# Another slot table and a longer lag between scores and values in a four-layer attention kernel

## The chip, the cores and the metric

The kernel runs on one core of a Trainium2 chip. The core has TensorE (PE; its weight loads are shown apart as PEld), VectorE (DVE), ScalarE (ACT), GpSimd (POOL) and SyncE (SP, which here issues the DMAs). The metric is the device time of one execution in microseconds; the median over several runs is compared.

## The reference

Four layers in a row on a 2048 x 576 input: multi-head attention A, multi-query attention B, A, B, each with a layer norm before it and a residual added behind it. There are 32 heads of 18 columns. In B all heads share one key and one value head.

```python
x = x + _A_ref(_layernorm(x), A_wqkv, A_wo)      # B: wq, and one wk, wv for all heads
...
scores = jnp.einsum("bhqd,bhkd->bhqk", q, k) * (Dh ** -0.5)
p = _softmax(scores, axis=-1)
o = jnp.einsum("bhqk,bhkd->bhqd", p, v)
return o.transpose(...).reshape(B, S, D) @ wo
```

## The kernel before

The order of all instructions is written out by hand (`manual_schedule`); each engine runs its own list in order, and semaphores hold an instruction until what it reads is there.

A layer has a projection part (queries, keys, values), an attention part and an output projection. The attention part goes through 16 pairs of heads and, in each pair, through four blocks of 512 queries: 64 units `w`, each for one `(p, u)`. The two heads of a pair, a = 0 and 1, use different row groups of PE, so a matmul of one and a matmul of the other run side by side.

A unit holds three strands of work:

- Maxima (`max_mm`, L563, and its matmuls L595). The scores of 128 queries against 512 keys are computed into one of three banks (`mtile`), and VectorE reduces each to a maximum (L602). To save reduces, some tiles are made in two steps: a "d" matmul (L587) gives the difference between two key blocks in one of four banks (`etile`), ACT writes its Relu into the scratch tile `side` (L592), and a later "t" matmul has VectorE add that and take the maximum (L599). When the 32 maxima of a block are there, `max_final` (L717) has VectorE take the negated maximum (`neg`, L719) and GpSimd split it in two parts (`hl`, L184 and L723); `max_store` (L725) has VectorE transpose the split (`tr`, L728) and SP store it, and `max_rows` (L732) has SP load it back as two more rows of the queries in `big`. These maxima are for a block about two units ahead.
- Exps (`exp_mm`, L737). A matmul (L743) gives 128 keys x 512 queries of scores with the maximum already subtracted, in one of the four `etile` banks, and ACT takes the exp (L749) into a score tile. Four of five score tiles come from a pool of 15 (`pt`); every fifth goes into one of three slices of `side` in turn (`side[:, 6 + n_p // 5 % 3]`).
- Values (`pv_cols` L753, `pv_block` L762, matmuls L770). Four score tiles are one block; a matmul of each with 19 columns of values and ones runs in its own column group, and eight blocks add up in the one bank `oacc`, which is then copied out (L184 or L182) and combined later: `o_sum` and `o_mul` on GpSimd, `l_part`, `l_out`, `l_rows`, `o_out` as DMAs on SP, `l_inv` on GpSimd. An fp32 value matmul stands in the profile as two passes.

The order of the three strands within a unit is the table `UNIT`, 32 slots, counted from 0. A slot such as "md" names what head 0 and head 1 do: "e" an exp tile, "m" a maximum, "d" and "t" the two-step maximum. The number behind a slot says how many columns of value work follow it; the slots between two numbers are called a group here, and the value work behind it a run. A unit has 16 exps and 16 maxima per head and 4096 columns of values. The value work trails the scores by `LAG` columns: at the start of a layer the first `LAG` columns are skipped, and they are made up behind the loop. `pv_cols` cuts a run wherever a block of 512 columns ends, and each piece is four matmuls of two passes.

The last unit but one goes by the table `ENDS`, the last by `LAST`. Work on a finished block, DMAs and loads are hung on stages: a stage is four exps of a head pair (eight stages in a unit), and `run_todo` (L844) issues what is due. `SUM_AT`, `NM_AT` and their like are offsets in stages. `CUT` says how many maxima of each head at the start of a unit still belong to the earlier block.

Of the kernel before, what the change touches and what calls it, by code (L numbers as in the profile page):

```python
# [45 lines left out]
LEAD = 14  # L46
NM_AT = 2
ROW_AT = 5
SUM_AT = 3
L_AT = 5  # L50
INV_AT = 8
R_AT = 8
# [9 lines left out]

UNIT = """md ee me 256 mm ee et 384 te em 320 me me ee 320 me em 384 em em md 448 ee em dt 448 me em em 384
          em te 256 me em ee 384 mm de me 384 me em 128"""
LAST = "ee ee 512 " * 8
LAG = 960

CUT = 4  # L70


def slots(text):
    out = []
    for w in text.split():
        if w.isdigit():
            out[-1][1] = int(w)
        else:
            out.append([w, 0])
    return out  # L80


UNIT, LAST = slots(UNIT), slots(LAST)
KINDS = [[w[a] for w, _ in UNIT if w[a] != "e"] for a in range(2)]
assert sum(n for _, n in UNIT) == 4096 and [len(k) for k in KINDS] == [16, 16]


def max_ops(kinds):
    pairs = kinds.count("d")
    rest = [(qc, kb) for qc in range(4) for kb in range(4) if qc >= pairs or kb > 1]  # L90
    seen, ops = {"d": 0, "t": 0}, []
    for k in kinds:
        if k == "m":
            ops.append((k, *rest.pop(0)))
        else:
            ops.append((k, seen[k], 0))
            seen[k] += 1
    assert not rest
    return ops


ENDS = UNIT[:8] + LAST[:10] + [["ee", 0], ["ee", 4096 - 5 * 512 - sum(n for _, n in UNIT[:8])]]
assert [[w[a] for w, _ in UNIT[:8]].count("e") for a in range(2)] == [8 - CUT] * 2
MAX_OPS = [max_ops(k[CUT:] + k[:CUT]) for k in KINDS]
PLAIN = [(i // 2 % 4, i // 8 % 2 * 2 + i % 2) for i in range(16)]
FIRST_SHARED = 3
# [3 lines left out]
def tile_kernel(ctx: ExitStack, tc: tile.TileContext, A_x, A_wqkv, A_wo, B_x, B_wq, B_wk, B_wv, B_wo, out):  # L110
# [66 lines left out]
    def xtile(name, shape=(P, 2, 9, 256), dt=F32R):  # L177
        return pool.tile(list(shape), dt, tag="xx", bufs=1, name=name)
# [223 lines left out]
    for layer in range(4):  # L402
# [350 lines left out]
        def pv_cols(cols):  # L753

            while cols:
                n, c0 = divmod(pv_at[0], 512)
                w = min(cols, 512 - c0)
                pv_block(n, c0, c0 + w)
                pv_at[0] += w
                cols -= w  # L760
# [54 lines left out]
        def at(b, f, *args):  # L815
            todo.setdefault(b, []).append((f, args))

        ns = STEPS * 4 * NPAIR
        for p in range(NPAIR):
            for u in range(4):  # L820
                b = STEPS * (4 * p + u) + STEPS - 1
                if is_a or p or u:
                    at(b + NM_AT, max_store, p, u)
                    at(b + ROW_AT, max_rows, p, u)
                for d, f in ((SUM_AT, o_sum), (L_AT, l_part), (INV_AT, l_inv), (R_AT, l_out), (RB_AT, l_rows),
                             (MUL_AT, o_mul), (O_AT, o_out)):
# [17 lines left out]
        def run_todo(st):  # L844
            for n in sorted(n for n in todo if n <= st):
                for f, args in todo.pop(n):
                    f(*args)
# [10 lines left out]
        side = xtile("side", (P, 9, 512), F32)  # L858
        late, n_e, n_r, n_p = LAG, 0, [0], [0]
        for w in range(4 * NPAIR):  # L860
            p, u = divmod(w, 4)
            more_m = w < 4 * NPAIR - 2
            e_next = [0, 0]
            for kinds, cols in UNIT if more_m else ENDS if w == 4 * NPAIR - 2 else LAST:
                run_todo(LEAD + STEPS * w + sum(e_next) // 4)
# [14 lines left out]
        for st in range(ns, ns + L_AT + 1):  # L880
            run_todo(LEAD + st)
            if st < ns + OUT_AHEAD:
                next(outs)
                pv_cols(LAG - 512 if st == ns else 512)
        tail = [todo.pop(n, []) for n in range(ns + LEAD + L_AT + 1, ns + LEAD + O_AT)]
# [32 lines left out]
```

## Time and profile before

| | us |
|---|---|
| median of 3 runs | 5732.63 (5728.56 to 5733.11) |
| profiled execution | 5727.82 |
| its span, first to last instruction | 5726.0 |
| PE busy | 5630.5 (98%) |
| VectorE busy | 4922.5 (86%) |
| ACT busy | 4890.3 (85%) |
| GpSimd busy | 1746.1 (30%) |

The profile is of one execution. Lines of a timeline have the start in us from the start of the span, the time that the merged instructions cover, the engine, the source line, what is written and read, and the count; in square brackets stands idle time of the engine before it, and what ended it. The granted TensorE clock was 0.998 of full speed over the span.

### The profile page before, as it was taken

What the parts mean: (1) busy time and instruction counts of PE and PEld (TensorE: products, weight loads), DVE (VectorE), ACT (ScalarE), POOL (GpSimd) and SP (SyncE); (2) the same over time, 40 slices, a digit from 0 to 9 for tenths busy, and PEclk for the clock granted to TensorE, in tenths of its full rate; (3) what the DMA queues carried; (4) which work ended last, traced back from release to release, by engine and by line L of the source; (5) the groups of instructions that cost most, each with busy time, mean ns of one, the idle gap of its engine ahead of it and who ended that gap; (6) DMA issues with size and microseconds to landing.
All of it is one profiled execution on the core that took longest, in us unless ns stands there. A gap on an engine that the chain in (4) does not pass through costs nothing.

```text
span 5726.0 us, 151306 instructions
## 1 busy us (share of the span) xinstructions
PE 5630.5 (98%) x59516; PEld 2991.4 (52%) x59516; DVE 4922.5 (86%) x9517; ACT 4890.3 (85%) x9864; POOL 1746.1 (30%) x2236
## 2 busy tenths in 40 slices
PE   9999999999999999999999999999999999999999
PEld 7644444444844444444685444444448444444446
DVE  4699999998699999999647999999977999999995
ACT  2499999999389999999625999999992899999996
POOL 3142323234233232333321332323342333333232
PEclk9999999999999999999999999999999999999999
DMA  6311111111320000001253111111114101010002
GB/s 226 112 44 39 35 39 36 39 36 25 126 68 23 23 21 22 20 23 25 59 193 93 49 36 37 36 38 39 33 37 127 55 23 24 23 24 20 21 16 78
DMA packets 258610, 292.42 MB, mean 51 GB/s; under 512 B 132700, under 2 KB 172892, under 8 KB 248176
## 3 DMA queue, kind: packets, MB, share of 16 engines
q1 hardware_dynamic: 257896, 282.75, 17.5%
q8 instruction: 467, 7.65, 0.6%
q14 instruction: 247, 2.02, 0.1%
HBM read 158.77 MB, written 119.86 MB: 49 GB/s over the span
## 4 chain that ended last, share of the span: by engine, by line
PE 90%; ACT 8%; DVE 1%; POOL 0%; issue 0%; DMA 0%; SPq 0%; DVEq 0%; ACTq 0%; POOLq 0%
PE oacc L770 36%; PE psm L595 22%; PE pse L743 19%; PE psn L262 6%; PE psq L421 6%; ACT pt L749 5%; PE psd L587 2%; ACT side L749 1%; ACT side L592 1%; DVE mx L602 0%; PE ps L254 0%; DMA qk_d<-ev 0%; POOL wsm L211 0%; PE oacc L255 0%; DVE oc L184 0%
## 5 line engine op out<-in xcount | busy, mean ns | idle before, releaser
L602 DVE TENSOR_REDUCE mxd<-psm 128x1 f32<-128x512 f32 x5856 | 3698.8, 683 | 263.2 <-PE psm L595 174.3
L749 ACT ACTIVATE pt<-pse 128x512 f32<-128x512 f32 x6580 | 3565.8, 635 | 156.5 <-PE pse L743 119.7
L595 PE MATMUL psm<-big 62*128 62x512 f32 x7216 | 2490.4, 447 | 7.0 <-DVE mx L602 5.6
L743 PE MATMUL pse<-big 64*128 64x512 f32 x8192 | 2424.5, 434 | 0.6 <-ACT evr L435 0.5
L770 PE MATMUL oacc<-pt,vbuf 128*19 128x192 f32 (+5 forms) x22768 | 1784.2, 356 | 4.1 <-DVE oc L184 3.6
L595 PEld LDWEIGHTS psm<-big 62*128 62x128 f32 x7216 | 1150.8, 184 | 848.9 <-DVE mxd L602 387.9
L743 PEld LDWEIGHTS pse<-big 64*128 64x128 f32 x8192 | 1202.4, 185 | 473.5 <-ACT pt L749 281.9
L770 PE MATMUL oacc<-side,vbuf 128*19 128x192 f32 (+6 forms) x5600 | 1321.3, 355 | 34.3 <-ACT side L749 31.7
L749 ACT ACTIVATE side<-pse 128x512 f32<-128x512 f32 x1612 | 1016.6, 631 | 24.0 <-PE pse L743 17.1
L770 PEld LDWEIGHTS oacc<-pt,vbuf 128*19 128x19 f32 x22768 | 571.2, 97 | 737.4 <-issue 578.4
L184 POOL TENSOR_SCALAR hl<-neg 128x8 fp32r<-128x8 f32 x256 | 50.9, 199 | 2809.4 <-DVE neg L719 2809.4
L599 DVE CUSTOM_DVE_ANT_0 side<-psm,side 128x512 f32<-128x512 f32 x976 | 650.9, 681 | 69.5 <-PE pse L743 64.2
L770 PE MATMUL oacc<-pt,vy 128*19 128x64 f32 (+2 forms) x8128 | 622.5, 343 | 0.0
L592 ACT ACTIVATE side<-psd 128x512 f32<-128x512 f32 x976 | 612.8, 628 | 0.0
L793 POOL TENSOR_TENSOR rl<-lt,mone 128x8 f32<-128x8 f32 x256 | 423.1, 1653 | 380.7 <-DMA lt<-os 380.7
L770 PEld LDWEIGHTS oacc<-side,vbuf 128*19 128x19 f32 x5600 | 363.2, 97 | 221.9 <-issue 136.3
L770 PE MATMUL oacc<-side,vy 128*19 128x192 f32 (+4 forms) x2000 | 438.2, 341 | 31.7 <-ACT side L749 31.7
L587 PE MATMUL psd<-kd,big 54*128 54x512 f32 x976 | 408.9, 419 | 0.0
L429 ACT ACTIVATE ev<-psq 128x512 fp32r<-128x512 f32 (+1 forms) x112 | 67.0, 598 | 325.8 <-PE psq L421 272.4
L806 POOL TENSOR_TENSOR os<-os,rb 96x512 f32<-96x512 f32 x256 | 328.7, 1284 | 19.1 <-DMA rb<-r_d 19.0
L784 POOL TENSOR_TENSOR os<-os,side 96x512 f32<-96x512 f32 x240 | 308.2, 1284 | 20.0
L770 PEld LDWEIGHTS oacc<-pt,vy 128*19 128x19 f32 x8128 | 198.9, 97 | 209.4 <-issue 177.0
(93 smaller groups left out, 3618.6 us busy)
## 6 DMA issues: line engine op xcount, KB each, us to landing
big<-qk_d SPq DMA_DIRECT2D x180, 432.0 KB
qk_d<-ev SPq DMA_DIRECT2D x96, 512.0 KB
qk_d<-ev SPq DMA_DIRECT2D x120, 256.0 KB
rb<-r_d SPq DMA_DIRECT2D x512, 36.0 KB
o_d<-os SPq DMA_DIRECT2D x512, 36.0 KB
m_d<-tr SPq DMA_DIRECT2D x1024, 2.0 KB
o<-o_d SPq DMA_DIRECT2D x64, 256.0 KB
big<-m_d SPq DMA_DIRECT2D x512, 4.0 KB
```

The costliest lines, as they stand in the source:

```text
L262: nc.tensor.matmul(ps, lhs[:, xc, :], wsm[:, wc, h * 288:(h + 1) * 288], start=i == 0, stop=i == len(TERMS) - 1)
L421: nc.tensor.matmul(ps[:n].rearrange("p (u t) -> p u t", u=2)[:, us], w[:, wc, :n], xts[T][:, us, xc, :], start=(xc, wc) == TERMS[0], stop= ...
L587: nc.tensor.matmul(ps, q[b:b + 3 * DH, c0:c0 + P], kds[p if is_a else 0][b:b + 3 * DH], start=True, stop=True)
L592: nc.scalar.activation(r, ps, AF.Relu)
L595: nc.tensor.matmul(ps, q[b:b + KM, c0:c0 + P], k[b:b + KM, kb * 512:(kb + 1) * 512], start=True, stop=True)
L599: nc.vector.tensor_tensor_reduce(out=r, in0=ps, in1=r, scale=1.0, scalar=-3.0e38, op0=OP.add, op1=OP.max, accum_out=mx[:, r0:r0 + 1])
L602: nc.vector.reduce_max(mx[:, r0:r0 + 1], ps, axis=AX.X)
L743: nc.tensor.matmul(e, k[r:r + KE, kc * P:(kc + 1) * P], q[r:r + KE, u * 512:(u + 1) * 512], start=True, stop=True)
L749: nc.scalar.activation(pt, e, AF.Exp, scale=SCALE)
L770: nc.tensor.matmul(oacc[j:j + DH + 1, cs], v_of(kc)[:, 2 * p + a if is_a else 0, :], pts[p, u, i][:, cs], start=kc < 2 and c0 == 0, stop=k ...
L793: nc.gpsimd.tensor_tensor(rl, lts.pop((p, u)), mone, op=OP.pow)
L806: nc.gpsimd.tensor_tensor(t[:96], t[:96], rb[:96], op=OP.mult)
```

## The change

Four things change together. `LAG` goes from 960 to 1152 columns. The slot table is another one, with the same number of each kind of slot: 16 exps, two "d", two "t" and twelve "m" per head, and twelve runs of value work. `SUM_AT` goes from 3 to 4, so that `o_sum` is issued one stage later. And `ENDS` is made by a function from the first ten slots of the table (`CUT_AT`), not from the first eight. As the change describes itself, no value run of the new table reads a score tile of the last four slots.

```diff
-SUM_AT = 3
+SUM_AT = 4
...
-UNIT = """md ee me 256 mm ee et 384 te em 320 me me ee 320 me em 384 em em md 448 ee em dt 448 me em em 384
-          em te 256 me em ee 384 mm de me 384 me em 128"""
+UNIT = """te ee 256 em me 384 et em me 512 et me ee 448 md dm em 384 em me 192 me ee me 192 md em 384
+          me me em 384 em ee te 192 mm ee 384 dm em em 384 me"""
 LAST = "ee ee 512 " * 8
-LAG = 960
+LAG = 1152

 CUT = 4
+CUT_AT = 10
...
-ENDS = UNIT[:8] + LAST[:10] + [["ee", 0], ["ee", 4096 - 5 * 512 - sum(n for _, n in UNIT[:8])]]
-assert [[w[a] for w, _ in UNIT[:8]].count("e") for a in range(2)] == [8 - CUT] * 2
+def ends(first):
+    left, cols = [16 - sum(w[a] == "e" for w, _ in first) for a in range(2)], 4096 - sum(n for _, n in first)
+    assert left[0] == left[1] and [sum(w[a] != "e" for w, _ in first) for a in range(2)] == [CUT] * 2
+    out = [list(x) for x in first]
+    for i in range(left[0]):
+        n = cols if i + 1 == left[0] else min(cols, 512) if i % 2 else 0
+        out.append(["ee", n])
+        cols -= n
+    return out
+
+
+ENDS = ends(UNIT[:CUT_AT])
```

## The prediction

> **What bounds the kernel.** I read the page first, then the busy time in windows, then PE's timeline, and VectorE's and GpSimd's beside it.
>
> ```profile
> span 5726.0 us, 151306 instructions
> PE 5630.5 (98%) x59516; PEld 2991.4 (52%) x59516; DVE 4922.5 (86%) x9517; ACT 4890.3 (85%) x9864; POOL 1746.1 (30%) x2236
> PE 90%; ACT 8%; DVE 1%; POOL 0%; issue 0%; DMA 0%; SPq 0%; DVEq 0%; ACTq 0%; POOLq 0%
> ```
> ```profile
> 1731.15:1826.13 94.98, 93.53 (x1087) 44.91 (x1080) 88.06 (x171) 91.92 (x186) 29.02 (x35) 1.00 0.09 20
> ```
>
> PE carries the chain, but in a stretch of five units (one unit is one pass through the table of 32 slots; the row has length, busy us of PE, PEld, DVE, ACT, POOL, granted clock, DMA) ACT is busy 97% and DVE 93%. So a unit is set by PE's own work plus the places where PE stands for ACT or DVE, and those have to be read one by one. PE's rows:
>
> ```profile
> 804.79 0.50 PE L595 MATMUL psm<-big 62*128 62x512 f32 x1
> ...
> 817.51 0.40 PE L743 MATMUL pse<-big 64*128 64x512 f32 x2
> ...
> 1733.44 0.42 PE L595 MATMUL psm<-big 62*128 62x512 f32 x1
> 1735.31 0.34 PE L770 MATMUL oacc<-side,vbuf 128*19 128x192 f32 x1 [1.45 <-ACT side L749]
> ...
> 1826.13 0.50 PE L595 MATMUL psm<-big 62*128 62x512 f32 x1
> ...
> 1838.10 0.51 PE L770 MATMUL oacc<-pt,vbuf 128*19 128x384 f32 x3
> 1838.76 0.23 PE L770 MATMUL oacc<-pt,vbuf 128*19 128x64 f32 x2
> 1838.99 0.50 PE L595 MATMUL psm<-big 62*128 62x512 f32 x1
> 1839.33 0.39 PE L595 MATMUL psm<-big 62*128 62x512 f32 x1
> 1839.56 0.39 PE L743 MATMUL pse<-big 64*128 64x512 f32 x1
> 1839.89 0.51 PE L770 MATMUL oacc<-pt,vbuf 128*19 128x384 f32 x2
> 1840.66 0.50 PE L743 MATMUL pse<-big 64*128 64x512 f32 x1
> 1841.32 0.23 PE L770 MATMUL oacc<-pt,vbuf 128*19 128x64 f32 x1
> ...
> 1841.88 0.49 PE L595 MATMUL psm<-big 62*128 62x512 f32 x1
> ...
> 1846.29 0.49 PE L595 MATMUL psm<-big 62*128 62x512 f32 x1
> ```
>
> From start to start: a group of three slots takes 0.34 + 0.23 + 0.33 = 0.90 us (1838.99 to 1839.89), one of two 0.66 us (1840.66 to 1841.32), a value run of 384 columns in one piece 0.77 us (1839.89 to 1840.66), one of 256 columns 0.56 us (1841.32 to 1841.88), one of 448 in two pieces 0.89 us (1838.10 to 1838.99); so a run is 0.14 us and 0.00164 us a column. The unit from 1826.13 to 1846.29 takes 20.16 us; taken out of the 94.98 us of five units, the plain ones are 18.70 us. The difference, 1.46 us, is the stand at 1735.31: 1733.44 to 1735.31 is 1.87 us where 0.33 is usual, so 1.54 us there. The view of waits has its kind in the first two lines (us in total, times, longest); the third is used at the end:
>
> ```profile
> PEld oacc L770 <- ACT side L749: 85.5, 73, 1.8
> PE oacc L770 <- ACT side L749: 63.4, 52, 1.5
> PEld psm L595 <- DVE mxd L602: 387.9, 732, 0.9
> ```
> ```profile
> 1734.61 0.65 ACT L749 ACTIVATE side<-pse 128x512 f32<-128x512 f32 x1
> ```
>
> PE waits for an exp that began at 1734.61, the newest one issued. Every fifth exp goes to one of three slices of side, so a slice is sent a new tile 15 exps later; by my count of the old table the run after slot 5 still reads columns 320 to 511 of a tile issued 15 exps before, so it waits for the exp that has just been given that slice. 32 exps a unit and every fifth to side make the pattern come round every five units.
>
> **The change, part by part.** A layer has 62 units by the table, four layers 248.
>
> *The stand.* In the new table the oldest tile that any run reads was issued 14 exps before, so no slice is rewritten under a reader, and by the counted distances no run needs an exp that is not four score tiles back, where the ring of four banks has already forced ACT to be done. 248 / 5 = 50 stands of 1.46 to 1.54 us go: −75 us. The next thing that can be late for a run, the copy of oacc, stands where it did.
>
> *Pieces.* 12 runs, 8 groups of three slots and 4 of two stay (the lone last slot joins the next unit's first two); cut at multiples of 512, the runs make 16 pieces instead of 19. From 384 columns in one piece to 448 in two is 0.12 us, and 64 columns are 0.105, so a further piece costs 0 to 0.02 us. I take 0.005, since starts are read to 0.01: 3 x 248 pieces are −4 us (0 to −15). The Trainium skill, "TensorE: Matmul & The Clock Gate", section "Wait — 56ns, not 53.3ns?", has a fixed 2.5 ns per matmul; a piece is eight matmuls, so that would be an estimated 20 ns and −15 us, and the sum 11 us lower. The rows above allow that only as their upper end.
>
> *VectorE.* The negated maximum (neg, L719) and the transpose of its split (tr, L728) move against the score maxima. Before, two reduces lie between them:
>
> ```profile
> 802.90 0.69 DVE L602 TENSOR_REDUCE mxd<-psm 128x1 f32<-128x512 f32 x1
> 803.62 0.19 DVE L719 TENSOR_REDUCE neg<-mxd 128x8 f32<-128x32 f32 x1
> 803.73 1.28 DVE L602 TENSOR_REDUCE mxd<-psm 128x1 f32<-128x512 f32 x2
> 804.92 0.20 DVE L728 STREAM_TRANSPOSE tr<-hl 128x32 f32<-128x32 f32 x1
> 805.33 0.69 DVE L602 TENSOR_REDUCE mxd<-psm 128x1 f32<-128x512 f32 x1 [0.20 <-PE pse L743]
> ...
> 823.86 0.20 DVE L728 STREAM_TRANSPOSE tr<-hl 128x32 f32<-128x32 f32 x1
> 824.00 1.29 DVE L602 TENSOR_REDUCE mxd<-psm 128x1 f32<-128x512 f32 x2
> ```
> ```profile
> 803.90 0.20 POOL L184 TENSOR_SCALAR hl<-neg 128x8 fp32r<-128x8 f32 x1 [11.26 <-DVE neg L719]
> 804.18 0.20 POOL L723 TENSOR_TENSOR hl<-neg,hl 128x8 fp32r<-128x8 f32 x1
> ```
> The transpose needs GpSimd's second hl, which ends at 804.38, 0.57 us after neg's end (803.81); the two reduces covered that. In the new table neg is issued after slot 8 and the transpose at slot 10 (12 exps issued, stage 3), and slot 9 is "ee": in the changed program's order nothing lies between them in 252 of 256 windows. So VectorE stands from 803.73, when neg lets it go on, to 804.42 (0.04 us after hl, an estimate from the 0.06 shown below for a freed bank): 0.69 us a unit, and every maximum behind it is late. No row of before shows VectorE standing there; that the reduces behind cannot pass the waiting transpose is what the Trainium skill says in "PSUM — Partial Sum Buffer", section "Engine vs sequencer instructions" (the queue is strict FIFO). By that rule the sum is as below; if they could pass, it would be the first rival's.
>
> What PE pays, with time 0 at the start of slot 7: PE is at slot 8 at 0.34, at slot 9 at 0.57, leaves for the 448-column run at 0.90, and is at slots 10, 11, 12 at 1.78, 2.12, 2.35, each with one maximum; the 384-column run from 2.68 ends at 3.46. VectorE starts slot 7's job at 0.54 (804.79 to 805.33), slot 8's at 1.14 (two reduces in a row take 1.29 and one 0.69, so a step is 0.60), neg at 1.86 (0.72, 802.90 to 803.62), which ends at 2.05; hl ends at 2.62, the transpose starts at 2.66 and slot 10's reduce at 2.80 (0.14, 823.86 to 824.00), ending at 3.49; slot 11's ends at 4.09. The ring of three maximum banks binds slot 13 to slot 10 and slot 14 to slot 11. What a freed bank costs is shown on ACT's side, in the first group of a unit:
>
> ```profile
> 1731.88 0.18 PEld L743 LDWEIGHTS pse<-big 64*128 64x128 f32 x1 [0.20 <-ACT pt L749]
> ```
> ```profile
> 1729.71 2.11 ACT L749 ACTIVATE pt<-pse 128x512 f32<-128x512 f32 x4
> ...
> 1732.21 0.59 ACT L749 ACTIVATE side<-pse 128x512 f32<-128x512 f32 x1
> 1732.69 0.60 ACT L749 ACTIVATE pt<-pse 128x512 f32<-128x512 f32 x1
> ```
> ```profile
> 1731.72 0.39 PE L595 MATMUL psm<-big 62*128 62x512 f32 x1
> 1731.88 0.49 PE L743 MATMUL pse<-big 64*128 64x512 f32 x1
> 1732.30 0.39 PE L770 MATMUL oacc<-pt,vbuf 128*19 128x256 f32 x1
> ```
>
> ACT's end 1731.82 to the weight load 1731.88 is 0.06 us, and the run follows 0.42 us later instead of 0.33, so 0.10 more when the load is not hidden. Slot 13 is due at 3.46 and can load at 3.49 + 0.06 = 3.55: 0.09 us. Slot 14 is then due at 3.89 and gets its bank at 4.09 + 0.16 = 4.25: 0.36 us. Together 0.45 us x 248 = +112 us. Bounds: 0, if VectorE's slack (6.9 of 94.98 us above) lay just here, and 0.69 x 248 = 171 us, if none did. I take 0.45, because both waits come out of the chain with durations that are in rows.
>
> *ACT.* In the first group above PE loses 1731.88 − 1731.72 = 0.16 and 0.09 us in the exit to ACT, 0.25 us in every unit. A score tile costs ACT 0.48 us (1732.21 to 1732.69). Tallying 0.48 per exp or Relu against the time of each group and run, with the copy of oacc as one more, ACT's backlog is highest at 0.84 us in the old table (the copy's 0.48, then "me me ee 320" brings four jobs, 1.92, in 0.90 + 0.66) and at 0.81 us in the new (0.24 left of the copy at slot 15, then "me ee me 192" brings 1.92 in 0.90 + 0.45). So I expect these waits at other places and of the same size, smaller by that 0.03 us: −7 us. Bounds: the largest single wait goes, or one more like it comes, ±0.25 x 248 = ±62 us.
>
> *SUM_AT, LAG, the ends.* o_sum goes one stage later on GpSimd, which is busy 30%, so the DMAs on SP behind it (lt, then o_d and the rows of maxima) may go up to 1.7 us later.
>
> ```profile
> 810.03 0.52 SPq L734 DMA_DIRECT2D big<-m_d x2
> ```
>
> The rows are issued 7.5 us before the unit's first exp that needs them (817.51), so that is covered. 192 more columns per layer move behind the loop: 192 x 0.00164 = 0.31 us, four times +1 us, if the loop's start gains nothing. The order of instructions on SP and GpSimd stays, and four oacc copies move from VectorE to ACT, 0.6 us each: nothing.
>
> Sum against the profiled execution, 5727.82 us (span 5726.0 and 1.8 around it; 4.8 us or 0.08% under the median of the runs, 5732.63, which I leave aside): 5727.8 − 75 − 4 + 112 − 7 + 1 = 5755 us.
>
> **Rivals.**
> 1. The removed stand pays and VectorE's hides (other side: faster). VectorE is idle 6.9 of 94.98 us, 1.4 us a unit, twice the 0.69. If the 0.69 us falls into that idle time and delays no bank, the sum loses the 112: 5643 us. Against it: in slots 10 to 14 five maxima follow in a row, and PE issues those slots faster than VectorE's 0.60 us each. It decides where the wait stays under 0.29 us a unit, (5716 − 5643) / 248.
> 2. Cost and gain cancel: a wait of 0.29 to 0.39 us a unit, 5716 to 5739 us.
> 3. VectorE's whole stand reaches PE, or PE's stand at a value run stays, at another place: 5643 + 171 = 5814 us, or 5755 + 75 = 5830 us. For it: VectorE is 93% busy. Against it: the distances counted above, and idle time of VectorE such as the 0.20 us before 805.33.
>
> **How the numbers follow.** The forecast's own case, a wait of 0.39 to 0.60 us, 5740 to 5792 us, gets 0.56; rival 1 0.16; rival 2 0.15; rival 3 0.13. About 0.2% (11 us) is what a measurement can tell from no change. Slower by more: the forecast's case and rival 3, with a little off for their edge, 0.67; within: 0.16; faster: 0.17. The range runs from 5700 to 5800 us: it holds the forecast's case, rival 2 and the edges of the others.
>
> **What would show it.** Right: no value run with idle time of a microsecond before it and a releaser on ACT; five-unit stretches all of one length, near 95.6 us (5 x (18.70 + 0.45 − 0.03 − 0.015)) instead of 94.98, with no long unit in them; VectorE idle before the transpose, about 0.6 us each and released by GpSimd's hl, some 150 us in all; PE's weight loads for maxima waiting for DVE some 100 us more than the 388 of before. Wrong: units of 18.3 to 18.7 us (rival 1), or a long unit every fifth (rival 3), or the first unit's exps waiting for rows of maxima.

## The result and the profile after

The changed kernel takes 5738.64 us (median of 17 runs, 5734.45 to 5745.97) against 5729.64 us (17 runs, 5724.97 to 5734.01) for the kernel before on the same chip: a ratio of 1.0016 with a 95% interval of 1.0009 to 1.0024. It is 9 us slower, inside the 0.2% that the prediction named as no change. The forecast was +27 us; the direction is right and the size is three times too large.

Lines of the changed kernel stand 13 further down than before (the score matmul L743 is L756 now, the value matmul L770 is L783, the exp L762, VectorE's reduce L615, its transpose L741). The page of the changed kernel:

```profile
span 5736.9 us, 139041 instructions
...
PE 5672.8 (99%) x53724; PEld 2800.5 (49%) x53724; DVE 4941.0 (86%) x9513; ACT 4951.8 (86%) x9868; POOL 1741.0 (30%) x2236
...
PE 74%; DVE 21%; POOL 2%; issue 1%; ACT 1%; DMA 0%; POOLq 0%; SPq 0%; DVEq 0%; ACTq 0%
```

The third line is the share of each engine in the chain that ended last. Before, it was PE 90%, ACT 8%, DVE 1%: beside PE, that chain now runs through VectorE and no longer through ScalarE. PE still waits for ScalarE too, as the table of groups below shows. The span grew by 10.9 us.

Busy time in two stretches of five units (start and end, length, then busy us of PE, PEld, DVE, ACT and POOL, granted clock, DMA share, GB/s):

```profile
777.78:872.89 95.11, 94.61 (x965) 41.13 (x961) 88.49 (x171) 93.18 (x187) 28.90 (x35) 1.00 0.15 37
872.89:967.99 95.10, 94.61 (x966) 41.13 (x962) 88.53 (x171) 93.16 (x187) 28.89 (x35) 1.00 0.15 37
```

Five units take 95.1 us, where they took 94.98 and the forecast was 95.6. No unit is long any more: over the 244 units whose twelve runs are all full, every one takes 18.91 to 19.12 us, mean 19.019; before, plain ones took 18.69 and every fifth about 20.2, mean 19.003.

The waits that the prediction spoke of (us in total, times, longest):

```profile
PEld psm L608 <- DVE mxd L615: 427.6, 1220, 0.7
...
PEld psm L608 <- DVE mxd L612: 177.5, 239, 0.7
...
DVE tr L741 <- POOL hl L736: 152.4, 252, 0.6
...
PE oacc L783 <- ACT side L762: 6.8, 4, 1.7
```

The stand of a value run behind a newly issued exp was 63.4 us in 52 places and is 6.8 us in 4. VectorE stands 252 times, 0.6 us each, before a transpose; that row did not exist before. Weight loads for maxima wait 605 us for VectorE's two kinds of reduce (the first two lines), 92 more than the 387.9 + 124.9 of before (the row that the prediction named, plain reduces alone, rose by 40).

One unit from slot 10 to the run behind slot 14, in the timeline of the changed kernel: VectorE first, then GpSimd, then PE and its weight loads (start, time covered, engine, line, what is written and read, idle time before it and what ended that):

```profile
783.83 0.69 DVE L615 TENSOR_REDUCE mxd<-psm 128x1 f32<-128x512 f32 x1
784.55 0.19 DVE L732 TENSOR_REDUCE neg<-mxd 128x8 f32<-128x32 f32 x1
785.35 0.21 DVE L741 STREAM_TRANSPOSE tr<-hl 128x32 f32<-128x32 f32 x1 [0.61 <-POOL hl L736]
785.48 2.44 DVE L615 TENSOR_REDUCE mxd<-psm 128x1 f32<-128x512 f32 x4
```
```profile
785.11 0.20 POOL L736 TENSOR_TENSOR hl<-neg,hl 128x8 fp32r<-128x8 f32 x1
```
```profile
784.43 0.50 PE L608 MATMUL psm<-big 62*128 62x512 f32 x1
...
784.96 0.18 PEld L756 LDWEIGHTS pse<-big 64*128 64x128 f32 x1 [0.23 <-ACT pt L762]
...
785.39 0.25 PE L783 MATMUL oacc<-pt,vbuf 128*19 128x64 f32 x3
...
786.17 0.50 PE L756 MATMUL pse<-big 64*128 64x512 f32 x1
...
786.78 0.18 PEld L608 LDWEIGHTS psm<-big 62*128 62x128 f32 x1 [0.42 <-DVE mxd L615]
...
787.22 0.35 PE L783 MATMUL oacc<-pt,vbuf 128*19 128x192 f32 x2
```

From the start of a group to the start of its run, slots 10 to 12 take 785.39 − 784.43 = 0.96 us, where three slots usually take 0.90, and slots 13 and 14 take 787.22 − 786.17 = 1.05 us, where two usually take 0.66. In the first of them ScalarE is late with one bank (784.96); in the second VectorE is late with the bank of slot 14 (786.78).

Read so for all 244 units, from start to start, the mean of each group of the new table (slots 31, 0 and 1 are the first, since the lone last slot joins the next unit's first two), beside those of three experiments that are told below:

| slots | usual | changed | NM_AT 3 | short exps | short exps, NM_AT 3 |
|---|---|---|---|---|---|
| 31, 0, 1 | 0.90 | 0.982 | 0.988 | 0.984 | 0.978 |
| 10 to 12 | 0.90 | 0.965 | 0.964 | 0.902 | 0.901 |
| 13, 14 | 0.667 | 1.042 | 0.664 | 1.103 | 0.668 |
| 15 to 17 | 0.90 | 0.901 | 1.044 | 0.901 | 0.979 |
| 18, 19 | 0.667 | 0.786 | 0.666 | 0.788 | 0.704 |
| 23 to 25 | 0.90 | 0.976 | 0.954 | 0.973 | 0.982 |
| unit | | 19.019 | 18.664 | 19.021 | 18.577 |

The other groups stand within 0.02 us of the usual.

### The profile page after: what moved, and what is told of

Same layout as the page of the kernel before. It is cut to its first block, busy times and chain, and to the rows that moved or that the text cites. A ratio compares the mean times of both kernels' runs of the same rounds, so it can differ in the third digit from the quotient of the medians.

```text
span 5736.9 us, 139041 instructions
## 1 busy us (share of the span) xinstructions
PE 5672.8 (99%) x53724; PEld 2800.5 (49%) x53724; DVE 4941.0 (86%) x9513; ACT 4951.8 (86%) x9868; POOL 1741.0 (30%) x2236
## 4 chain that ended last, share of the span: by engine, by line
PE 74%; DVE 21%; POOL 2%; issue 1%; ACT 1%; DMA 0%; POOLq 0%; SPq 0%; DVEq 0%; ACTq 0%
PE oacc L783 26%; PE psm L608 18%; PE pse L756 16%; DVE mxd L615 13%; PE psn L275 6%; PE psq L434 6%; DVE side L612 6%; PE psd L600 2%; DVE tr L741 1%; POOL hl L736 1%; DVE neg L732 1%; POOL hl L197 1%; DVE mx L615 1%; PE ps L267 0%; POOLq L197 0%
## 5 line engine op out<-in xcount | busy, mean ns | idle before, releaser
L615 DVE TENSOR_REDUCE mxd<-psm 128x1 f32<-128x512 f32 x5856 | 3645.1, 681 | 129.8 <-PE pse L756 46.6
L762 ACT ACTIVATE pt<-pse 128x512 f32<-128x512 f32 x6580 | 3588.3, 622 | 110.6 <-PE pse L756 58.7
L608 PE MATMUL psm<-big 62*128 62x512 f32 x7216 | 2619.9, 453 | 30.6 <-DVE mx L615 5.0
L756 PE MATMUL pse<-big 64*128 64x512 f32 x8192 | 2465.5, 434 | 4.4 <-ACT pt L762 2.7
L783 PE MATMUL oacc<-pt,vbuf 128*19 128x64 f32 (+6 forms) x20492 | 1797.6, 377 | 3.8 <-DVE oc L197 3.6
L756 PEld LDWEIGHTS pse<-big 64*128 64x128 f32 x8192 | 1213.1, 185 | 904.8 <-ACT pt L762 538.3
L783 PE MATMUL oacc<-side,vbuf 128*19 128x64 f32 (+6 forms) x5044 | 1408.5, 376 | 6.8 <-ACT side L762 6.8
L762 ACT ACTIVATE side<-pse 128x512 f32<-128x512 f32 x1612 | 999.9, 620 | 18.7 <-PE pse L756 7.1
L783 PEld LDWEIGHTS oacc<-pt,vbuf 128*19 128x19 f32 x20492 | 454.2, 97 | 618.2 <-issue 504.7
L605 ACT ACTIVATE side<-psd 128x512 f32<-128x512 f32 x976 | 591.6, 649 | 0.0
L783 PE MATMUL oacc<-pt,vy 128*19 128x384 f32 (+3 forms) x5756 | 587.6, 415 | 0.0
L783 PE MATMUL oacc<-side,vy 128*19 128x384 f32 (+2 forms) x1412 | 456.0, 414 | 0.0
L783 PEld LDWEIGHTS oacc<-side,vbuf 128*19 128x19 f32 x5044 | 319.8, 97 | 157.3 <-issue 124.6
L197 POOL TENSOR_SCALAR os<-side 32x512 f32<-32x512 f32 x480 | 293.6, 612 | 40.0 <-POOL hl L736 0.2
```

The costliest lines, as they stand in the source:

```text
L197: eng.tensor_scalar(dst, src, 1.0, 0.0, op0=OP.mult, op1=OP.add)
L605: nc.scalar.activation(r, ps, AF.Relu)
L608: nc.tensor.matmul(ps, q[b:b + KM, c0:c0 + P], k[b:b + KM, kb * 512:(kb + 1) * 512], start=True, stop=True)
L615: nc.vector.reduce_max(mx[:, r0:r0 + 1], ps, axis=AX.X)
L756: nc.tensor.matmul(e, k[r:r + KE, kc * P:(kc + 1) * P], q[r:r + KE, u * 512:(u + 1) * 512], start=True, stop=True)
L762: nc.scalar.activation(pt, e, AF.Exp, scale=SCALE)
```

## The experiments

**The VectorE stand alone, in the changed kernel.**

```diff
-NM_AT = 2
+NM_AT = 3
```

> The changed kernel with the transpose of the maxima one stage later (NM_AT 3), so that reduces lie between neg and the transpose again. Theory A (VectorE's stand before the transpose makes PE wait at slots 13 and 14, and PE's other waits are ACT's ring of four): the stand of 0.6 us goes, the group of slots 13 and 14 falls from 1.04 to about 0.67 us, some 0.05 of it comes back at ACT's waits, units of 18.64 to 18.75 us instead of 19.02, time 5645 to 5672 us. Rival B (the terms of the prediction simply add up, 0.45 us a unit for VectorE): 5627 us. Rival C (the wait at slots 13 and 14 is ACT's, and VectorE's stand is hidden): 5738 us, no change.

Measured 5649.08 us, ratio to the kernel before 0.9862 (0.9848 to 0.9877): Theory A, and not the 5627 us at which the terms of the prediction would simply add up (Rival B). Slots 13 and 14 fall to 0.664 us, so the whole excess of 0.375 us in that group was VectorE's stand at the transpose. The unit falls by 0.355 us. Behind that group the waits mostly change places: slots 15 to 17 take 0.14 us more, slots 18 and 19 take 0.12 us less. The gain is 88 us.

**The same stand in the old table.**

```diff
-NM_AT = 2
+NM_AT = 1
```

> The kernel before with the transpose one stage earlier (NM_AT 1): in the old table, too, no reduce lies between neg (after slot 7) and the transpose (at slot 8). Theory A: VectorE stands 0.6 to 0.7 us before each transpose, the maxima of slots 8, 9, 11 and 12 are late, and PE pays 0.40 to 0.65 us a unit: 5830 to 5890 us. Rival C (VectorE's 1.4 us of idle time a unit hide the stand): 5730 us.

Measured 5854.67 us, 1.022 (1.0203 to 1.0237), in Theory A's range. The row of the stand appears in the view of waits with nearly the count and length that it has in the changed kernel:

```profile
DVE tr L728 <- POOL hl L723: 151.1, 250, 0.6
```

Plain units go from 18.69 to 19.23 us, so here it costs PE 0.54 us a unit. A transpose too close behind its neg costs 0.36 us a unit in the new table and 0.54 in the old one.

**The stand of the value run alone, in the old table.**

```diff
-            own = n_p[0] % 5 or (p, u) == (NPAIR - 1, 3)
-            pt = pts[p, u, i] = ptile("pt") if own else side[:, 6 + n_p[0] // 5 % 3]
+            own = n_p[0] % 6 or (p, u) == (NPAIR - 1, 3)
+            pt = pts[p, u, i] = ptile("pt") if own else side[:, 6 + n_p[0] // 6 % 3]
```

> The kernel before with every sixth instead of every fifth score tile in the three slices of side, so that a slice is given a new tile 18 exps later and the run after slot 5 reads the tile itself (before, it read the last 192 columns of such a tile from the slice already given to the tile 15 exps later). Theory A (PE's 1.5 us every fifth unit is the wait for the exp just given to that slice): no long units, all at 18.69 us, 5655 us (5645 to 5665). Rival D (ACT is simply that far behind at slot 5 in such units): long units stay, 5725 to 5735 us.

Measured 5649.79 us, 0.9863 (0.9848 to 0.9878), 77 us less than before. A slice of `side` is now sent a new tile 18 exps later, and the long units are gone, five in a row taking 93.41 us instead of 94.98:

```profile
1860.68:1954.09 93.41, 93.41 (x1086) 44.99 (x1080) 87.96 (x171) 91.78 (x186) 28.92 (x35) 1.00 0.09 20
```

So the stand was the rewritten slice, and taking it away is worth what the prediction put down for it. The stand is also a sign of something else: once in five units the kernel before takes, for 192 columns of one score tile, the newer exp that PE has waited for and not the tile that belongs there. The old table with this one edit and the new table with NM_AT 3 are 77 us and more under both kernels, and level with each other.

**The lag alone, backwards.**

```diff
-LAG = 1152
+LAG = 960
```

> The changed kernel with LAG 960, as before: the new table alone. The oldest tile read is then 12 exps old, so no slice is rewritten under a reader; runs read tiles that are as little as 3 exps old. Theory A: no long units, VectorE's stand and the wait at slots 13 and 14 stay, tiles 3 exps old are ready: units of 19.02 us plus 0.01 for more pieces, 5730 to 5745 us. Rival E (the longer lag pays by itself, because fresh score tiles make runs wait for ACT): 0.1 us a unit and more, 5760 us or over.

Measured 6032.18 us, 1.0532 (1.0516 to 1.0547): the main expectation missed by 290 us. One run does it, the 512 columns behind slots 4 to 6, which take 2.21 us instead of 0.99 in every unit. PE and ScalarE there:

```profile
815.98 0.43 PE L783 MATMUL oacc<-pt,vy 128*19 128x320 f32 x1
817.42 0.35 PE L783 MATMUL oacc<-pt,vbuf 128*19 128x192 f32 x3 [1.01 <-ACT side L195]
```
```profile
816.27 0.60 ACT L762 ACTIVATE pt<-pse 128x512 f32<-128x512 f32 x1
816.75 0.62 ACT L195 ACTIVATE side<-oacc 128x512 f32<-128x512 f32 x1
```

With 960 columns a head's last block ends 320 columns into that run. The remaining 192 columns begin the next sum in `oacc`, so they wait for the copy of `oacc` (L195), and the copy stands in ScalarE's queue behind the exps of slots 4 to 6. With 1152 = 256 + 384 + 512 columns the block ends where the run ends, and the copy goes on under the next group's scores. The old table has the same fit at 960 = 256 + 384 + 320. The lag is therefore part of the table, not a choice beside it. The prediction had said that the copy "stands where it did", which is so, but it had priced the lag by the 192 columns at the ends of a layer alone and not seen that the new table needs the longer lag for that.

**The lag alone, in the old table.** To see whether that holds there too:

```diff
-SUM_AT = 3
+SUM_AT = 4
...
-LAG = 960
+LAG = 1152
```

> The kernel before, its old slot table, with LAG 1152 and SUM_AT 4: the lag alone. By the count of the old table a block of 512 columns then ends inside a 320-column run, not at a run's end. Theory A (what the lag has to fit is the copy of oacc: where a block ends inside a run, PE waits there for ScalarE's copy, 1.22 us a unit as in the changed kernel with LAG 960): 1.1 to 1.3 us a unit, +270 to +320 us, and with the stands at rewritten slices kept or up to doubled 6000 to 6130 us. Theory B (the copy is hidden in this table, and the lag only moves which exps a run reads): 5640 to 5830 us, by whether the stands go or double.

Measured 6277.05 us, 1.0953 (1.0934 to 1.0971). Two runs of the table read a slice of `side` here after a newer exp was written into it, where one does in the kernel before, so a larger part of the values is summed from other scores; the time is read for the waits. PE's own (us, times, longest):

```profile
PE oacc L770 <- ACT side L182: 384.3, 240, 1.8
PE oacc L770 <- ACT side L749: 85.1, 104, 1.5
```

The run with the block's end in it, 320 columns behind slots 8 to 10, takes 2.56 us in the mean instead of 0.67, once a unit, and the stands at rewritten slices double from 52 to 104. The mechanism of Theory A is there; its size was put 150 us too low, for that run loses 1.9 us a unit here and not 1.2 (and the granted clock was 0.983 over this span, not 0.998).

**A lighter ScalarE.** The prediction had tallied ScalarE's waits as a backlog of exps and Relus. In the changed kernel, with a zeroed tile for the columns that are not written:

```diff
-                nc.scalar.activation(r, ps, AF.Relu)
+                nc.scalar.activation(r[:, :64], ps[:, :64], AF.Relu)
...
+        nc.gpsimd.memset(side[:, 0:4], 0.0)
```

> The changed kernel with ScalarE made lighter: its Relu of a d tile covers only the first 64 of 512 columns, and the other columns of those slices stay zero, so the maxima of a fifth of the tiles are wrong. Four Relus a unit, two of them in slots 10 and 11, one in 18 and one in 28. Theory A (the waits for ScalarE and for VectorE in slots 10 to 14 overlap: where ScalarE holds PE at slot 12, slot 13 no longer waits): without the Relus the group of slots 10 to 12 falls from 0.965 to 0.90 us, and the group of slots 13 and 14 rises from 1.042 to 1.09 to 1.13 us, near the 0.667 + 0.45 of the prediction. Theory B (the two waits are independent and their sum is paid): slots 10 to 12 fall to 0.90 and slots 13 and 14 stay at 1.03 to 1.05. Both: the first group of a unit loses its 0.085 us and the unit is 18.85 to 18.95 us in A (5695 to 5720 us), 18.78 to 18.86 in B (5678 to 5698).

Measured 5736.49 us, 1.0014 (1.0004 to 1.0023), level with the changed kernel, against both theories. ScalarE's Relus, in the view of groups (busy us and mean ns, then idle time before):

```profile
L605 ACT ACTIVATE side<-psd 128x64 f32<-128x64 f32 x976 | 224.7, 271 | 0.0
```

They take 224.7 us instead of 591.6, and the unit falls by 0.013 us. Slots 10 to 12 stay at 0.965 and slots 13 and 14 at 1.041. The reason is in ScalarE's rows of the changed kernel:

```profile
782.85 0.60 ACT L195 ACTIVATE side<-oacc 128x512 f32<-128x512 f32 x1
783.34 1.57 ACT L762 ACTIVATE pt<-pse 128x512 f32<-128x512 f32 x3
784.77 0.63 ACT L762 ACTIVATE side<-pse 128x512 f32<-128x512 f32 x1
785.25 1.14 ACT L605 ACTIVATE side<-psd 128x512 f32<-128x512 f32 x2
```

Slot 12's exp uses the bank of the first exp of slot 9, four tiles back; that one ends at 784.91, behind the copy and the exps of slots 7 and 8, and the weight load follows at 784.96. The Relus of slots 10 and 11 come behind it in the queue and cannot matter. ScalarE's idle time took the rest. So this run did not test what it was meant to test.

**The light Relu with NM_AT 3**, where the same two edits go together:

> The same kernel with the short Relu and with NM_AT 3, so that the transpose is two groups further behind the negated maximum. Theory A (overlap): the edit is worth more here than the 88 us it is worth with the full Relu, 95 to 115 us, because the 0.067 us of ScalarE's wait no longer cover a part of VectorE's: 5590 to 5620 us. Theory B (independent): the same 88 us, 83 to 93, so 5595 to 5610 us when the short Relu alone gives 5690.

Measured 5639.13 us, 0.9847 (0.9832 to 0.9862), above both ranges, as the light Relu alone had been. The step between the two is 97 us. Theory A's range for that step holds it, but the gain has another place than A gave: slots 10 to 12 stay at 0.964, while slots 15 to 17 fall from 1.044 to 0.982 us and slots 18 and 19 rise from 0.666 to 0.702.

**The transpose one stage later still.**

```diff
-NM_AT = 2
+NM_AT = 4
```

> The changed kernel with NM_AT 4 in place of 2, one stage later than the 3 already measured at 5649 us. With 3 the group of slots 15 to 17 took 1.044 us instead of 0.902. Theory A (what is left at NM_AT 3 in slots 15 to 17 is VectorE at the transpose): that group falls to 0.90 to 0.95 us, and the wait, if VectorE stands elsewhere, appears where the transpose now is; the unit is 18.53 to 18.68 us, 5615 to 5655 us. Theory B (it is ScalarE's backlog from the copy of oacc and four jobs in short time): that group stays at 1.03 to 1.05 us, and the time at 5640 to 5655 us. Rival C: the rows of maxima come too late for their exps with the later store, and PE stands for a DMA: over 5700 us.

Measured 5652.77 us, 0.987 (0.9855 to 0.9884). Slots 15 to 17 stay at 1.044 us, with the transpose elsewhere. So it is not VectorE that takes 0.14 us there, but ScalarE (Theory B).

**The copy of `oacc` on VectorE**, with NM_AT 3 and then with NM_AT 2:

```diff
-                copy(nc.scalar if m_done[0] < 4 * ns else nc.vector, oc, oacc)
+                copy(nc.vector, oc, oacc)
```

> The changed kernel with NM_AT 3 and the copy of oacc always on VectorE, where 240 of 256 are on ScalarE. The work is the same. Theory A (what is left of waits at NM_AT 3, 0.35 us a unit, is mostly ScalarE's backlog behind the copy): slots 15 to 17 fall from 1.044 us towards 0.90, and the time is 5600 to 5640 us. Rival B (VectorE, busier by 0.6 us a unit, makes the maxima late instead): 5660 to 5800 us, with more idle time of PE's weight loads behind VectorE's reduces.

> The changed kernel (NM_AT 2) with the copy of oacc always on VectorE. With NM_AT 3 this edit took ScalarE's wait out of slots 10 to 12 (0.902 us instead of 0.964), while slots 7 to 9 took 1.231 us. Theory A (slots 10 to 14 share one delay: VectorE's chain fixes when slot 14 can go, and what ScalarE takes at slot 12 is not paid again): slots 10 to 12 take 0.90 and slots 13 and 14 take 1.09 to 1.13 us instead of 1.042, together 2.00 to 2.02 as in the changed kernel (0.965 + 1.042 = 2.007). Theory B (independent waits): 0.90 and 1.03 to 1.05, together 1.94. The time is 5780 to 5805 us in A and 5765 to 5785 in B, worked out from the 5708 us with NM_AT 3 and one group of 0.37 to 0.44 us a unit more, less 0 to 0.1 us that ScalarE gains by it.

With NM_AT 3: 5708.39 us, 0.9966 (0.9953 to 0.9978). ScalarE's waits shrink (slots 10 to 12 at 0.902, 15 to 17 at 0.979), but the run behind slots 7 to 9 waits 0.33 us. The time is in Rival B's range, but what PE waits for is the copy itself and not a late maximum (us, times, longest):

```profile
PE oacc L783 <- DVE side L197: 62.4, 240, 0.3
```

With NM_AT 2: 5867.42 us, 1.0241 (1.0226 to 1.0257), some 70 us over both theories. Slots 10 to 12 take 0.902, but slots 13 and 14 take 1.293 us. In VectorE's rows the copy stands ahead of the two maxima that neg needs:

```profile
798.47 0.68 DVE L197 TENSOR_SCALAR side<-oacc 128x512 f32<-128x512 f32 x1
799.07 0.68 DVE L612 CUSTOM_DVE_ANT_0 side<-psm,side 128x512 f32<-128x512 f32 x1
799.67 0.09 DVE L612 DVE_READ_ACCUMULATOR2_ANT mxd<- 128x1 f32 x1
799.67 0.69 DVE L615 TENSOR_REDUCE mxd<-psm 128x1 f32<-128x512 f32 x1
800.40 0.19 DVE L732 TENSOR_REDUCE neg<-mxd 128x8 f32<-128x32 f32 x1
801.19 0.21 DVE L741 STREAM_TRANSPOSE tr<-hl 128x32 f32<-128x32 f32 x1 [0.61 <-POOL hl L736]
```

Slot 10 starts at 800.09 in this unit, so neg is 0.31 us behind it, where it was 0.12 us in the changed kernel (784.55 and 784.43). Every bank behind the transpose comes that much later, and PE pays 1.293 − 0.667 = 0.63 us of a stand that is as long as before. The run moved VectorE's start and so says nothing of the two theories that it was made for. It shows that neg 0.19 us later makes the same stand 0.19 us dearer for PE, 0.63 us instead of the 0.44 that the next two experiments give for it in the changed kernel.

**ScalarE's wait at slot 12 alone.** This one takes away what makes ScalarE late there, and leaves VectorE and GpSimd as they are:

```diff
+    half = cst.tile([P, 512], F32, name="half")
+    nc.gpsimd.memset(half, 0.0)
...
-        return pool.tile(list(shape), dt, tag="p", bufs=15, name=name)
+        return pool.tile(list(shape), dt, tag="p", bufs=14, name=name)
...
-            pt = pts[p, u, i] = ptile("pt") if own else side[:, 6 + n_p[0] // 5 % 3]
-            nc.scalar.activation(pt, e, AF.Exp, scale=SCALE)
+            short = i in (8, 10)
+            pt = pts[p, u, i] = half if short else ptile("pt") if own else side[:, 6 + n_p[0] // 5 % 3]
+            w = 256 if short else 512
+            nc.scalar.activation(pt[:, :w], e[:, :w], AF.Exp, scale=SCALE)
```

> The changed kernel with the two exps of slots 7 and 8 cut to 256 of 512 columns, into a tile of their own whose other half stays zero (so a part of the weights of two score tiles a unit is left out); the ring of score tiles has 14 instead of 15. It takes away what makes ScalarE late at slot 12, and touches neither VectorE nor GpSimd's hl. Theory A (slots 10 to 14 share one delay, VectorE's chain): slots 10 to 12 fall from 0.965 to 0.90 us and slots 13 and 14 rise from 1.042 to 1.08 to 1.13, their sum stays at 1.99 to 2.02 and the time within 10 us of the changed kernel's 5737. Theory B (independent waits): 0.90 and 1.03 to 1.05, the sum 1.94, and 5712 to 5725 us.

> The same two short exps with NM_AT 3, so that the transpose stands clear of slots 10 to 14. Both theories: slots 10 to 12 at 0.90 us and slots 13 and 14 at 0.667, so the short exps gain 0.06 us a unit here, 5630 to 5640 us instead of 5649. In A the step from NM_AT 2 to 3 is then worth 100 to 110 us with the short exps, 88 with the full ones; in B it is worth 80 to 92 with both.

Measured 5737.67 us, 1.0018 (1.0009 to 1.0028), level with the changed kernel although 0.4 us of ScalarE's work per unit is gone. PE's rows (in this kernel the value matmul is L787):

```profile
782.96 0.50 PE L610 MATMUL psm<-big 62*128 62x512 f32 x1
...
783.86 0.25 PE L787 MATMUL oacc<-pt,vbuf 128*19 128x64 f32 x3
...
784.64 0.50 PE L758 MATMUL pse<-big 64*128 64x512 f32 x1
784.71 1.09 PE L610 MATMUL psm<-big 62*128 62x512 f32 x2
785.31 0.49 PE L758 MATMUL pse<-big 64*128 64x512 f32 x1
785.73 0.35 PE L787 MATMUL oacc<-pt,vbuf 128*19 128x192 f32 x2
```

Slots 10 to 12 take 0.90 us, and slots 13 and 14 now 1.09: slot 13's maximum starts 0.07 us behind its exp (784.64 and 784.71), which it did not in the changed kernel (786.17 and 786.18). In the mean over 244 units it is 0.902 + 1.103 = 2.005 us, where the changed kernel has 0.965 + 1.042 = 2.007. With NM_AT 3 and the same short exps the time is 5629.40 us, 0.9827 (0.9812 to 0.9841): NM_AT is worth 108 us here and 88 us with full exps. Both numbers are Theory A's: what ScalarE takes at slot 12 is not paid again at slot 13.

The run of the new table with `LAG` 960 shows the same, and it shortens no exp. There the copy of `oacc` is done before slot 7 begins, so ScalarE is not late at slot 12. Slots 10 to 12 take 0.899 us and slots 13 and 14 take 1.109, together 2.008.

## Why the prediction was right in direction and too large in size

The sum by its own terms, against what the traces give over the 244 full units (4 fewer than the 248 of the prediction). "Groups" are the scores' share of a unit and "runs" the values', without the long stand:

| term | predicted, us | measured, us | from |
|---|---|---|---|
| stands of the value run | −75 | −76 | 49 long units of before, mean 0.313 us a unit |
| pieces | −4 | −4 | runs of a unit 8.441 to 8.426 us |
| VectorE | +112 | +108 | 2.005 − 1.564 (the usual 0.90 and the 0.664 of NM_AT 3) = 0.441 us a unit in slots 10 to 14, with ScalarE out of the way; the 1.569 of the short exps with NM_AT 3 would give 106 us |
| ScalarE's waits | −7 | −24 | all groups of a unit 10.249 to 10.593 us, +84, less the 108 |
| outside the full units | +1 | +7 | the rest of the span |
| sum | +27 | +11 | span 5726.0 to 5736.9 us |

- *The stand.* Right in place, cause and price, and nothing took its place at a value run. Undoing it alone in the old table gave the same 77 us.
- *Pieces.* Three pieces fewer save 15 ns a unit, 5 ns each, as taken. The fixed 2.5 ns per matmul of the Trainium skill, "TensorE: Matmul & The Clock Gate", section "Wait — 56ns, not 53.3ns?", times eight matmuls would have been 20 ns; the two traces do not show that for value matmuls, which run in four column groups side by side. If the four groups pay it at the same time, that figure of the Trainium skill gives an estimated 5 ns for two passes; no run here tests that.
- *VectorE.* Right. Counted from slot 7's start (782.65), neg starts at 1.90, the transpose at 2.70 and the next reduce at 2.83 us, where the prediction had 1.86, 2.66 and 2.80. The stand is 0.61 us long, 252 times (0.69 from where the prediction began to count it, while neg still runs), and the reduces do stay behind the waiting transpose, as the Trainium skill has it in "PSUM — Partial Sum Buffer", section "Engine vs sequencer instructions". PE's 0.45 us a unit is measured as 0.441 where ScalarE is not late ahead of it.
- *ScalarE's waits on top of VectorE's: the step that failed.* The prediction said that ScalarE's waits come "at other places and of the same size, smaller by that 0.03 us", and added them to VectorE's 0.45 in full. Alone they have about that size: with NM_AT 3 the groups of a unit exceed the usual by 0.37 us together, where those of before exceed it by 0.38. Beside VectorE's stand they add only 0.28 us. The 0.065 us at slot 12 falls in a stretch that VectorE's chain has already fixed: PE comes later to slot 13 and finds its bank just freed, so the 0.09 us put down for slot 13 is not paid. The 0.36 us put down for slot 14 is paid (0.375). 0.065 x 244 = 16 us is nearly all of the difference between −7 and −24. The short exps and `LAG` 960 show this. The slots 15 to 19 show the like on a smaller scale, where ScalarE's 0.14 us of NM_AT 3 is 0.12 us one group later in the changed kernel, behind VectorE's stand.
- *What the split of the two terms means.* Which of the two is charged with the overlap is a choice of the table. It prices VectorE's stand alone (+108) and leaves the rest to ScalarE (−24). Priced by taking NM_AT to 3 in the changed kernel, VectorE's stand is worth 88 us, and ScalarE's term comes out near its −7. Each term was right by itself; their addition was wrong, by some 20 us.
- *Where ScalarE's waits come from.* The tally of exps and Relus as one backlog gave about their sum and not their cause. Some 60% of the Relu work could go without moving the time; each wait hangs on the exps just ahead of one bank.
- *The ends.* +7 instead of +1. The 192 columns are 1 us of it. What the other 6 us are was not settled; no run was made for it, nor one for `SUM_AT` or the new `ENDS` alone.
- *The length of five units.* The sum in brackets behind the 95.6 us of the prediction comes to 95.5; 95.1 were measured.
- *The rivals.* The time falls where the second rival put it, 5716 to 5739 us. VectorE's wait alone, 0.441 us, lies in the forecast's own 0.39 to 0.60; what PE saves without it in the changed kernel, 0.355 us, lies in that rival's 0.29 to 0.39, because of the overlap. The first rival is refuted by either number, the third by the trace: no long units, and 0.61 us of stand that do not all reach PE. The copy put on VectorE shows that 0.63 us can.

## What to carry to other kernels

Waits of one engine for two others need not add up. Each pushes the waiting engine later, and what the other has ready by then is free, so follow one chain of times through the stretch in which both lie, and price an engine's lateness against the later of the two. When a table of slots moves, look where a store or transpose stands behind the value that it needs, and where a block ends within a run; in this kernel either of them costs more than the stand that the change was made of, and one offset (NM_AT) makes a version that is 1.4% faster than the one and 1.5% faster than the other.

## What the runs showed that was not expected

The copy of `oacc` is hidden only because a block ends where a run ends: 192 columns of lag to either side cost 1.2 us a unit in the new table and 1.9 us in the old one. Taking 367 us of busy time from ScalarE, at 86% one of the fullest engines, moved the time by some 2 us, and by 10 us with NM_AT 3. And the same 0.61 us stand of VectorE cost PE 0.44 or 0.63 us a unit in the new table, by how late VectorE was when it came to it, and 0.54 us in the old one, at other slots. The rule that each microsecond of lateness is passed on whole rests on that one pair.
